# A gated-attention and feed-forward kernel on one core: its written-out order of work replaced by another, with four filler products fewer at the start

## The chip, the cores and the metric

The kernel runs on one core of a Trainium2 chip. The core has a matrix engine (PE; its weight loads are shown apart as PEld), a vector engine (DVE), an activation engine (ACT), a general engine (POOL), a queue that issues the transfers (SP), and 16 DMA engines that carry them out. The metric is the time of one execution on the device, in microseconds (us).

## What is computed

The first half is a recurrent attention over 768 steps for 4 batches of 8 heads of width 48, with a decay alpha per step and channel; the second is a feed-forward layer over the 3072 tokens (width 384, hidden width 2048) with the ELU function in between. Cut to what matters:

```python
for t in range(S):
    state = alpha[:, :, t, :, None] * state + einsum('bhd,bhe->bhde', k[:, :, t], v[:, :, t])
    y[:, :, t] = einsum('bhd,bhde->bhe', q[:, :, t], state)
x = y.transpose(0, 2, 1, 3).reshape(B * S, H * D)      # 3072 x 384
h = x @ w_in                                           # 3072 x 2048
g = np.where(h > 0, h, exp(minimum(h, 0)) - 1)
out = g @ w_out                                        # 3072 x 384
```

## The kernel before

**Windows.** The 768 steps of a batch are cut into six windows of 128 steps, 24 windows in all. In each the products of the decays are made by a scan, and the recurrence becomes a few small matrix products: scores of the queries and keys within a window, masked, and the state that is carried from window to window. The results are the columns of x.

**Token blocks and hidden blocks.** The feed-forward layer runs over nine blocks b of tokens: b = 0 to 2 have 256 tokens (two windows), b = 3 to 8 have 384 (three windows). Over the hidden width it runs in pieces j (8 of 256 columns for the first three b, 16 of 128 after that). Each 32-bit operand of these products is split into a high and a low part, and a product is made of three: high with high, high with low, low with high.

**An order written out by hand.** Every step of the program is a function with a short name (a token), and the string ORDER lists some 1,640 of them; the program is emitted in that order. Each engine carries out its own steps strictly in that order, and a step waits until what it reads is there and until the buffer that it writes is free. Two more strings say which buffers: BANKS gives, token by token, which of the eight PSUM banks a product writes, SLOTS which of eleven slots of a ring (128x512 each) holds a tile of the feed-forward layer or an output tile. A slot that held an output tile is free when the DMA that writes the output has landed. Four sets (WLV, KAV, KBV, SQV) name the windows or weights whose step runs on DVE and not on POOL, and GQ the blocks whose GL step runs on POOL and not on DVE.

The tokens that the change and the prediction's steps touch, with lines of the kernel before:

| token | engine, line | what it does |
|---|---|---|
| X.n.k, and the call X(WARM) | PE, L209 | n products of a constant tile, read by nobody (fillers); WARM of them run ahead of everything |
| L.i, LA.i, LB.i, LV.i | SP, L260 to L288 | load keys, queries and decays of window i (L whole, LA the decays, LB the rest), LV its values; the tiles for L are three, taken in turn |
| SC.i, LN.i, EX.i | DVE L300, ACT L312, L318 | scan of the decays, its logarithm, the exponential of its negative |
| KA.i, KB.i, KC.i | DVE or POOL L326, L331, DVE L336 | keys divided by the decay product, with one correction step |
| PC.i | ACT, L341 | a sum for the final check |
| TP.i (T.i later), KN.i | PE L379, ACT L409 (T: DVE L389) | transpose the keys; KN copies the result out of PSUM |
| SQ.i, S.i, MK.i | DVE or POOL L354, L357; PE L444, L428; DVE L461, L456 | queries times decays, scores, mask |
| U.i, UA.i, UB.i, UC.i | PE L491, L473; ACT L508 or DVE L510; DVE L510; DVE L539, L541 | the window's addition to the state, and the state for its second half and the next window |
| YL.i, Y3.i, Y.i, XH.i, XP.i, XL.i | PE L552, L606, L557; ACT L594, L621; PE L625; ACT or DVE | the window's results and their split into high and low |
| F.f, KW, DA, DB, WH.f, WL.f | SP L676; ACT L687; DVE L703, L708; ACT L735; DVE or POOL L755 | load weight tile f as 64-bit words, make 32-bit values of them, split these (KW, DA and DB by a pair of tiles) |
| A.b.j | PE, L787 | h for token block b and hidden piece j |
| RA, RB, RC, GH, GL (b.j) | ACT L796, L801; DVE L807; ACT L813; POOL or DVE L820 | ELU of h, its high part gh and its low part gl |
| O.b.j | PE, L836 | adds the piece's share to the output products o |
| Z.b.m | ACT L846, SP L849 | copies o out of PSUM into a ring slot, and issues the output's DMA |

The last step compares a few sums and leads to a slow general version if the inputs are out of the range for which the fast one holds; that is the same in both.

Of the kernel before, what the change touches and what calls it, by code (L numbers as in the profile page):

```python
# [61 lines left out]
YL.1 Y3.1 XP.0 Y.1 WH.2 XL.0 WH.0 F.6 MK.2 YL.2 KA.3 KB.3 KC.3 TP.3 WL.0 XH.1 KN.3 XP.1 XL.1 S.3 WL.2 F.4 KW.2 F.3
DA.2 Y3.2 LV.3 A.0.0 KW.1.1 RA.0.0 DA.1.1 F.7 F.1 DB.2 WH.6 WL.6 UB.2 DB.1.1 Y.2 XH.2 U.3 L.5 MK.3 F.5 UC.2 UA.3 PC.3
A.0.1 YL.3 WH.4 WL.4 KW.1.0 DA.1.0 RB.0.0 RC.0.0 DB.1.0 SC.5 RA.0.1 GH.0.0 UB.3 GL.0.0 L.4 RB.0.1 Y3.3 F.8 WH.1 A.0.3
RA.0.3 WL.1 WH.3 WL.3 XP.2 XL.2 F.10 RB.0.3 RC.0.1 Y.3 XH.3 LV.7 RC.0.3 UC.3 XL.3 KW.3 A.0.2 DA.3 SC.4 LN.5 A.1.1 DB.3
RA.0.2 RB.0.2 RA.1.1 EX.5 KA.5 O.0.0 RB.1.1 A.1.0 KW.4 RC.0.2 RC.1.1 RA.1.0 RB.1.0 GH.0.1 GL.0.1 GH.0.2 LN.4 F.12 DA.4
DB.4 WH.10 RC.1.0 GH.1.0 LC.1 A.1.3 KB.5 GL.1.0 WH.7 WH.8 WL.7 GH.1.1 F.9 GL.0.2 GL.1.1 A.1.2 O.0.1 RA.1.2 RB.1.2
WL.10 EX.4 O.1.0 CA.1 RC.1.2 KA.4 WH.5 WL.8 O.1.1 GH.1.2 WL.5 RA.1.3 RB.1.3 GL.1.2 A.1.5 RC.1.3 GH.0.3 F.14 ZV.6 KW.6
DA.6 CB.1 F.11 A.0.4 O.1.2 RA.0.4 RB.0.4 A.0.5 RA.1.5 O.0.2 KB.4 DB.6 WH.14 GL.0.3 SQ.4 KC.4 S.4 WH.12 RB.1.5 RA.0.5
RC.0.4 L.6 KC.5 RC.1.5 DA.5 GH.0.4 KW.5 LV.6 MK.4 TP.4 RB.0.5 GH.1.5 RC.0.5 KN.4 TP.5 KN.5 LC.3 DB.5 GH.1.3 O.0.3 PC.4  # L70
SQ.5 CA.3 LV.5 U.5 WH.9 WL.12 S.5 MK.5.1 MK.5.0 A.0.6 WH.11 WL.11 CB.3 RA.0.6 GL.1.3 O.1.3 LV.4 U.4 RB.0.6 RC.0.6 PC.5
SC.6 WL.9 LN.6 EX.6 GL.0.4 A.1.4 RA.1.4 RB.1.4 UA.4 UB.4 UC.4 L.7 SC.7 LN.7 KA.6 LC.2 RC.1.4 WL.14 A.1.6 KB.6 A.1.7
UA.5 GH.0.5 O.0.4 EX.7 KA.7 KB.7 RA.1.7 KC.6 RA.1.6 RB.1.7 RC.1.7 F.13 GH.1.4 GH.0.6 Y.5 RB.1.6 KC.7 T.7.2 GL.1.5 XH.5
Y.4 PC.7 RC.1.6 XH.4 XL.4 TP.6 GL.1.4 O.1.4 KN.6 F.15 DA.7 KW.7 O.1.5 U.6 UA.6 XL.5 DB.7 PC.6 SQ.6 S.6 MK.6.1 CA.2
GH.1.6 WH.13 GL.0.5 O.0.5 GH.1.7 L.8 UB.6 UC.6 XD.5 WL.13 GL.0.6 XD.4 LV.9 SC.8 WH.15 WL.15 MK.6.0 A.0.7 RA.0.7 GL.1.6
CB.2 RB.0.7 LN.8 EX.8 KA.8 A.2.1 T.7.3 RC.0.7 KB.8 T.7.0 KC.8 T.8.3 T.8.0 O.0.6 T.8.2 L.9 GH.0.7 A.2.0 RA.2.0 RB.2.0
LC.0 GL.1.7 O.1.6 O.1.7 Z.1.0 Z.1.1 GL.0.7 O.0.7 Z.0.0 LV.8 A.2.2 RC.2.0 RA.2.1 RB.2.1 T.7.1 GH.2.0 Z.0.1 SQ.7 U.7
RC.2.1 RA.2.2 GH.2.1 PC.8 S.7 UA.7 SQ.8 UB.7 MK.7.0 UC.7 RB.2.2 RC.2.2 GL.2.1 CA.0 S.8 SC.9 LN.9 T.8.1 EX.9 L.11 Y.6
MK.8.1 XH.6 MK.7.1 A.2.5 RA.2.5 XL.6 XD.6 GL.2.0 A.2.6 A.2.4 RA.2.4 MK.8.0 A.2.3 RB.2.5 RC.2.5 KA.9 KB.9 U.8 UA.8 Y.7
LV.11 RA.2.6 Y.8 RB.2.6 SQ.9 CB.0 GH.2.2 GL.2.2 RB.2.4 KC.9 UB.8 UC.8 GH.2.5 TP.9 KN.9 RC.2.6 XH.8 XL.8 XH.7 O.2.0  # L80
XL.7 GL.2.5 A.2.7 RC.2.4 RA.2.7 SC.11 SQ.11 U.9 LN.11 EX.11 S.9 MK.9.1 MK.9.0 RB.2.7 RC.2.7 UA.9 UB.9 UC.9 LV.10 XD.8
# [1016 lines left out]
```

## Time and profile before

| | us |
|---|---|
| median of 3 runs (464.18 to 464.94) | 464.34 |
| the profiled execution | 465.35 |
| its span, from the first to the last instruction | 463.5 |

| engine | busy us | share of the span | instructions |
|---|---|---|---|
| PE | 456.1 | 98% | 4948 |
| PEld | 440.3 | 95% | 4948 |
| DVE | 349.7 | 75% | 756 |
| ACT | 327.6 | 71% | 741 |
| POOL | 214.2 | 46% | 185 |

The span and the time of the execution differ by what lies ahead of the first and behind the last instruction. Busy time says how long an engine had an instruction in it; products on PE overlap, so the pitch from one to the next tells more than their length. In rows of the trace "out<-in" names the tile that is written and those that are read, "xN" says how many equal instructions were merged, and "[0.60 <-DVE ...]" that the engine was idle for 0.60 us just before and what ended that.

### The profile page before, as it was taken

What the parts mean: (1) busy time and instruction counts of PE and PEld (TensorE: products, weight loads), DVE (VectorE), ACT (ScalarE), POOL (GpSimd) and SP (SyncE); (2) the same over time, 40 slices, a digit from 0 to 9 for tenths busy, and PEclk for the clock granted to TensorE, in tenths of its full rate; (3) what the DMA queues carried; (4) which work ended last, traced back from release to release, by engine and by line L of the source; (5) the groups of instructions that cost most, each with busy time, mean ns of one, the idle gap of its engine ahead of it and who ended that gap; (6) DMA issues with size and microseconds to landing.
All of it is one profiled execution on the core that took longest, in us unless ns stands there. A gap on an engine that the chain in (4) does not pass through costs nothing.

```text
span 463.5 us, 12462 instructions
## 1 busy us (share of the span) xinstructions
PE 456.1 (98%) x4948; PEld 440.3 (95%) x4948; DVE 349.7 (75%) x756; ACT 327.6 (71%) x741; POOL 214.2 (46%) x185
## 2 busy tenths in 40 slices
...
GB/s 256 415 411 286 306 103 159 150 157 104 90 236 10 172 116 178 123 49 138 47 176 139 126 66 179 155 70 154 78 120 35 121 45 52 34 35 85 35 4 57
DMA packets 23715, 61.10 MB, mean 132 GB/s; under 512 B 3040, under 2 KB 10720, under 8 KB 23648
## 3 DMA queue, kind: packets, MB, share of 16 engines
...
q10 hardware_dynamic: 432, 0.59, 0.3%
...
## 4 chain that ended last, share of the span: by engine, by line
PE 88%; ACT 5%; DVE 4%; issue 1%; DMA 1%; POOL 0%; DVEq 0%; ACTq 0%; POOLq 0%
PE h L787 38%; PE o L836 38%; PE y L557 4%; PE q L428 2%; PE q L473 2%; PE wp L209 1%; PE y L552 1%; ACT w L735 1%; DVE raw L703 1%; DMA out_dram<-ot 1%; DVE wm L708 1%; ACT gh L813 1%; ACT r L801 1%; ACT r L796 1%; PE y L606 1%
## 5 line engine op out<-in xcount | busy, mean ns | idle before, releaser
L787 PE MATMUL h<-xt,w 128*128 128x384 f32 (+1 forms) x1296 | 200.1, 310 | 0.3 <-DVE r L807 0.3
L787 PEld LDWEIGHTS h<-xt,w 128*128 128x128 f32 x1296 | 190.8, 190 | 1.5 <-DVE r L807 0.4
L836 PE MATMUL o<-w,gh 128*128 128x384 f32 x768 | 188.4, 327 | 0.0
L820 POOL TENSOR_TENSOR gl<-r,gh 128x384 fp32r<-128x384 f32 (+1 forms) x90 | 106.4, 1189 | 158.7 <-ACT gh L813 104.9
L836 PEld LDWEIGHTS o<-w,gh 128*128 128x128 f32 x768 | 134.0, 189 | 0.5
L836 PE MATMUL o<-w,gl 128*128 128x384 f32 x384 | 125.3, 326 | 0.2 <-POOL gl L820 0.2
L796 ACT ACTIVATE r<-h 128x384 f32<-128x384 f32 (+1 forms) x120 | 60.5, 510 | 55.8 <-PE h L787 49.3
L389 DVE STREAM_TRANSPOSE kn<-qka 32x128 f32<-32x128 f32 x256 | 77.5, 303 | 4.2
L807 DVE SCALAR_TENSOR_TENSOR r<-r,h 128x384 f32<-128x384 f32 (+1 forms) x90 | 51.0, 577 | 38.0 <-ACT r L801 31.4
L836 PEld LDWEIGHTS o<-w,gl 128*128 128x128 f32 x384 | 72.6, 189 | 0.6 <-POOL gl L820 0.5
L801 ACT ACTIVATE r<-r 128x384 f32<-128x384 f32 (+1 forms) x120 | 64.1, 543 | 2.0
L813 ACT CAST gh<-r 128x384 fp32r<-128x384 f32 (+1 forms) x90 | 46.4, 528 | 18.6 <-DVE r L807 16.1
L357 POOL TENSOR_TENSOR st<-qka,P 64x512 f32<-64x512 f32 x34 | 43.0, 1265 | 17.4 <-DVE P L300 16.1
L456 DVE TENSOR_TENSOR st<-q,mask 64x256 f32<-64x256 f32 x76 | 32.1, 422 | 9.2 <-PE q L428 6.0
L326 POOL TENSOR_TENSOR qka<-qka,R 128x512 f32<-128x512 f32 x16 | 21.1, 1316 | 29.9 <-ACT R L318 27.8
L807 DVE SCALAR_TENSOR_TENSOR h<-r,h 128x384 f32<-128x384 f32 (+1 forms) x30 | 17.5, 589 | 21.0 <-ACT r L801 20.5
L300 DVE TENSOR_TENSOR_SCAN P<-qka,first 128x516 f32<-128x516 f32 (+1 forms) x25 | 31.0, 1244 | 0.5 <-DMA qka<-in_qka_dram 0.2
L820 DVE TENSOR_TENSOR gl<-h,gh 128x384 fp32r<-128x384 f32 (+1 forms) x30 | 17.3, 582 | 18.2 <-ACT gh L813 7.7
L726 ACT ACTIVATE ck<-ck,lim 128x384 f32<-128x384 int32 x32 | 25.5, 795 | 0.6
L721 ACT ACTIVATE ck<-ck,lim 128x384 int32<-128x384 int8 x32 | 25.3, 792 | 0.0
L312 ACT ACTIVATE R<-P 128x512 f32<-128x512 f32 (+1 forms) x25 | 15.4, 615 | 11.4 <-DVE P L300 11.3
L813 ACT CAST gh<-h 128x384 fp32r<-128x384 f32 (+1 forms) x30 | 14.8, 497 | 8.8 <-DVE h L807 7.2
...
## 6 DMA issues: line engine op xcount, KB each, us to landing
qka<-in_qka_dram SPq DMA_DIRECT2D x18, 770.0 KB, 5.5
...
```

The source lines that it names most:

```text
L300: nc.vector.tensor_tensor_scan(out=P[:, n].rearrange("p n w -> p (n w)"), data0=t[:, 2 * NP * W + n.start * AW:2 * NP * W + n.stop * AW], ...
L357: eng(SQV, i).tensor_tensor(out=st[r, a], in0=d["q"][r], in1=pw(i)[r], op=ALU.mult)
L389: nc.vector.transpose(out=kn[32 * t:32 * t + 32, :, 32 * g:32 * g + 32], in_=d["kt"][32 * g:32 * g + 32, :, 32 * t:32 * t + 32])
L456: nc.vector.tensor_tensor(out=d["st"][r, a, :, c * C:(c + 1) * C], in0=d["s4"][a][o], in1=mask[o].unsqueeze(1).broadcast_to([64, NP, C]), ...
L726: nc.scalar.activation(out=t[:, :, 1].bitcast(F32), in_=t[:, :, 0], func=AF.Square, bias=lim[:, 1:2], accum_out=chk_w[:, f:f + 1])
L787: nc.tensor.matmul(h[:, y, :], lhsT=t[:, wi, ws], rhs=x[:, c, xi].rearrange("p (a x) -> p x a", a=2), start=(y == 0 and k == 0), stop=(k = ...
L796: nc.scalar.activation(out=r, in_=d["h"], func=AF.Relu, scale=-1.0)
L801: nc.scalar.activation(out=d["r"], in_=d["r"], func=AF.Exp, scale=-1.0)
L807: nc.vector.scalar_tensor_tensor(out=d["g"], in0=d["r"], scalar=-1.0, in1=d["h"], op0=ALU.add, op1=ALU.max)
L813: nc.scalar.copy(out=gh, in_=d["g"])
L820: q.tensor_tensor(out=gl, in0=d["g"], in1=d["gh"].bitcast(F32), op=ALU.subtract)
L836: nc.tensor.matmul(o[:, 0:DM], lhsT=gt[:, y, ms], rhs=t[:, wi, f * DM:f * DM + DM].rearrange("p (a x) -> p x a", a=2), start=(u == 0 and y ...
```

## The change

WARM goes from 17 to 13. ORDER, BANKS and SLOTS are replaced as a whole, and the sets that divide work between DVE and POOL are replaced with them. The functions are the same. The new ORDER is one line longer, which shifts the code below it by one: L326 before is L327 after. Of the tables a line or two:

```diff
-WARM = 17
+WARM = 13
...
-WLV, KAV, KBV, SQV = (0, 2, 7, 8, 10, 11, 13, 15),  \
-    (0, 1, 2, 3, 6, 7, 14, 22),  \
-    (0, 1, 2, 3, 4, 7, 11, 22, 23),  \
-    (0, 1, 18, 19)
+WLV, KAV, KBV, SQV = (0, 7, 8, 10, 11, 13, 15),  \
+    (0, 1, 2, 3, 7, 14, 18, 19, 22, 23),  \
+    (0, 1, 2, 3, 4, 6, 7, 22, 23),  \
+    (0, 1, 18, 21, 23)
...
 ORDER = """
-LA.0.0 SC.0.0 LN.0.0 EX.0.0 LA.0.1 SC.0.1 LB.0.0 LN.0.1 KA.0.0 LV.0.0 KB.0.0 EX.0.1 KC.0.0 TP.0.0 KA.0.1 KB.0.1 KC.0.1
-PC.0 X.4.1 TP.0.1 KN.0 LA.1 SC.1 LB.1.1 LB.0.1 LN.1 X.4.2 U.0 SQ.1 SQ.0 EX.1 S.0 LB.1.0 KA.1 KB.1 KC.1 X.2.0 UC.0 L.2
+LA.0.0 SC.0.0 LN.0.0 EX.0.0 LA.0.1 SC.0.1 LB.0.0 LA.1 KA.0.0 KB.0.0 LN.0.1 KC.0.0 EX.0.1 KA.0.1 KB.0.1 TP.0.0 LV.0.0
+X.4.1 KC.0.1 PC.0 LB.1.1 LB.0.1 TP.0.1 KN.0 X.3.2 U.0 SC.1 SQ.1 LN.1 LB.1.0 SQ.0 S.0 EX.1 KA.1 KB.1 X.2.0 KC.1 PC.1
...
 BANKS = """
-7012345671205364721567305216401732542014564164514514516545614561420763542107563475423616142302147350
+7012345671205364721563407521632475603247517417547574517457415757415326041726053760475317542312476302
...
 SLOTS = """
-0123456789a042356718904625783a6918a0564904672013a56829734a065872130694a27565704981324756243185706967
+0123456789a135607241a5690738146a928a17595a16039247a815629738a15420683249a754a12349608297824076934671
```

What this moves, at three places. The names are those of the program; a number behind a tile's name only tells tiles apart.

SP, the queue of transfers, from the first weight tiles on. qka is the input of a window (L), vs the values (LV; 128x384 is a half), raw a weight tile (F). Before:

```order
L676 DMA raw_278<-in_wgt_dram 128x6141 x2
L260 DMA qka_128<-in_qka_dram 128x1540
L285 DMA vs_114<-in_vv_dram 128x768
L285 DMA vs_113<-in_vv_dram 128x384
L676 DMA raw_432<-in_wgt_dram 128x6141 x2
L676 DMA raw_478<-in_wgt_dram 128x6141
L285 DMA vs_115<-in_vv_dram 128x768
```

After:

```order
L677 DMA raw_282<-in_wgt_dram 128x6141 x2
L261 DMA qka_124<-in_qka_dram 128x1540
L286 DMA vs_109<-in_vv_dram 128x384
L286 DMA vs_110<-in_vv_dram 128x768
L677 DMA raw_437<-in_wgt_dram 128x6141
L286 DMA vs_111<-in_vv_dram 128x768
L677 DMA raw_437<-in_wgt_dram 128x6141
L677 DMA raw_454<-in_wgt_dram 128x6141
```

L.3 (the second row) keeps its place; the half LV.1.1 and LV.2 behind it change places, and LV.3 moves up between the weight tiles F.4 and F.6.

DVE, from the state of window 2 to the keys of window 3. P is the scan of window 3, wm the weights of pair 0, st the masked scores and vs the state of window 2. Before:

```order
L541 SCALAR_TENSOR_TENSOR vs_114<-u,P 128x192
L703 TENSOR_SCALAR raw_278<-raw_278 128x768
L708 SCALAR_TENSOR_TENSOR wm<-raw_278 128x768
L300 SCALAR_TENSOR_TENSOR P<-qka_128,first 128x516
L708 SCALAR_TENSOR_TENSOR wm<-raw_278 128x768
L510 TENSOR_TENSOR vs_114<-vs_114,q 128x192
L461 TENSOR_TENSOR st<-sc,mask 128x2x4x64
L326 TENSOR_TENSOR qka_128<-qka_128,R 128x512
```

After:

```order
L542 SCALAR_TENSOR_TENSOR vs_110<-u,P 128x192
L709 SCALAR_TENSOR_TENSOR wm<-raw_282 128x768
L704 TENSOR_SCALAR raw_282<-raw_282 128x768
L301 SCALAR_TENSOR_TENSOR P<-qka_124,first 128x516
L462 TENSOR_TENSOR st<-sc,mask 128x2x4x64
L511 TENSOR_TENSOR vs_110<-vs_110,q 128x192
L709 SCALAR_TENSOR_TENSOR wm<-raw_282 128x768
L327 TENSOR_TENSOR qka_124<-qka_124,R 128x512
```

The number of steps ahead of the scan (SC.3) and of the keys (KA.3) is the same; the state step (UA.2) now stands ahead of the second weight step, and the mask (MK.2) ahead of both.

ACT, from the results of windows 4 and 5 (y, xt) to the state of window 6 (vs). kn is the copy of window 6's transposed keys, raw with 128x1536 the cast of weight pair 7. Before:

```order
L620 ACTIVATE y_1367,chk_y<-y 128x128
L621 ACTIVATE xt,chk_y<-y 128x3x128
L409 COPY kn<-tp 128x512
L687 ACTIVATE raw_1296<-raw_1296 128x1536
L508 ACTIVATE vs_114<-q 48x192 x2
```

After:

```order
L621 ACTIVATE y_1360,chk_y<-y 128x128
L622 ACTIVATE xt,chk_y<-y 128x3x128
L814 CAST gh<-r 128x512
L688 ACTIVATE raw_1325<-raw_1325 128x1536
L410 COPY kn<-tp 128x512
L509 ACTIVATE vs_110<-q 48x192 x2
```

A gh and the cast of the weight pair now stand ahead of the copy of the keys.

## Rows read from the trace of the kernel before

**Rows 1.** Stages: us; busy us (instructions) by engine; granted clock; DMA share; GB/s.
```profile
15.00:20.00 5.00, 5.00 (x106) 4.41 (x106) 4.83 (x9) 4.46 (x12) 1.05 (x1) 1.00 1.02 407
...
60.00:70.00 10.00, 10.00 (x102) 9.71 (x102) 9.98 (x9) 9.09 (x14) 9.34 (x6) 1.00 0.45 120
```

**Rows 2.** The chain that ended last: start us, us, what.
```profile
1.07 6.78 PE wp L209 x17
...
451.57 7.33 PE o L836 x45
```

**Rows 3.** PE's waits: us in total, times, longest us.
```profile
PE tp L379 <- DVE qka L336: 0.6, 1, 0.6
PE y L606 <- ACT y L594: 0.3, 1, 0.3
PE h L787 <- DVE r L807: 0.3, 1, 0.3
PE q L473 <- DMA vs<-in_vv_dram: 0.3, 1, 0.3
PE o L836 <- POOL gl L820: 0.2, 1, 0.2
```

**Rows 4.** PE's weight loads in order of time: start us, us.
```profile
7.02 0.34 PEld L209 LDWEIGHTS <-wz 128*128 128x128 bf16 x2 [0.28 <-issue]
7.48 0.36 PEld L379 LDWEIGHTS tp<-ident,qka 128*128 128x128 f32 x2
```

**Rows 5.** DVE in order of time: KC.0.0, KC.0.1, SC.3, DB.0.0, KA.3, KC.3.
```profile
6.01 0.42 DVE L336 SCALAR_TENSOR_TENSOR qka<-R,qka 128x256 f32<-128x256 f32 x1
...
7.27 0.42 DVE L336 SCALAR_TENSOR_TENSOR qka<-R,qka 128x256 f32<-128x256 f32 x1
...
20.23 1.23 DVE L300 TENSOR_TENSOR_SCAN P<-qka,first 128x516 f32<-128x516 f32 x1
21.38 0.93 DVE L708 SCALAR_TENSOR_TENSOR wm<-raw 128x768 int32<-128x768 int32 x1
...
23.09 0.81 DVE L326 TENSOR_TENSOR qka<-qka,R 128x512 f32<-128x512 f32 x1
...
24.66 0.69 DVE L336 SCALAR_TENSOR_TENSOR qka<-R,qka 128x512 f32<-128x512 f32 x1
```

**Rows 6.** PE in order of time: TP.1, U.2, TP.3, the first h behind S.3.
```profile
13.30 0.66 PE L379 MATMUL tp<-ident,qka 128*128 128x128 f32 x4 [0.60 <-DVE qka L336]
...
21.27 0.68 PE L473 MATMUL q<-vs,kn 64*64 64x48 f32 x32 [0.27 <-DMA vs<-in_vv_dram]
...
25.83 0.66 PE L379 MATMUL tp<-ident,qka 128*128 128x128 f32 x4
...
27.66 2.27 PE L787 MATMUL h<-xt,w 128*128 128x256 f32 x18
```

**Rows 7.** SP in order of time: the issue of L.3.
```profile
12.21 0.33 SPq L260 DMA_DIRECT2D qka<-in_qka_dram  x1
```

**Rows 8.** Transfers issued from 12.2 to 12.4 us: count, KB each, us to landing.
```profile
qka<-in_qka_dram SPq DMA_DIRECT2D x1, 770.0 KB, 8.0
```

**Rows 9.** Line L849, the output's transfers from 313 to 325 us.
```profile
DMA to landing us min/median/max: 1.9/4.1/4.3
```

**Rows 10.** ACT and PE in order of time: two gh, kn.6, KW.7; U.6.
```profile
85.93 1.14 ACT L813 CAST gh<-r 128x512 fp32r<-128x512 f32 x2
...
90.26 0.58 ACT L409 COPY kn<-tp 128x512 f32<-128x512 f32 x1
90.73 2.45 ACT L687 ACTIVATE raw<-raw 128x1536 int32<-128x1536 uint8 x1
...
93.91 0.57 PE L473 MATMUL q<-vs,kn 64*48 64x48 f32 x32
```

**Rows 11.** PE in order of time: the last o ahead of an island of small products.
```profile
334.35 0.33 PE L836 MATMUL o<-w,gl 128*128 128x384 f32 x1
334.61 0.57 PE L473 MATMUL q<-vs,kn 64*48 64x48 f32 x32
```

More of the change, by code (lines that the diff above doesn't have):

```diff
@@ L62 @@
[L62 to L81, printed above, removed]
@@ new lines @@
+A.1.3 RC.1.0 KA.5 KB.5 RB.1.1 RC.1.1 GL.0.2 WH.8 GH.1.0 LN.4 GL.1.0 O.0.0 O.0.1 WH.10 WL.10 O.1.0 GH.1.1 GL.1.1 O.1.1
+EX.4 KA.4 RB.1.2 RC.1.2 RA.1.3 RB.1.3 WH.7 GH.1.2 WL.8 WH.5 WL.7 LV.7 GL.1.2 RC.1.3 LC.1 CA.1 WL.5 KB.4 ZV.6 LV.4 CB.1
+F.14 KW.6 LV.6 SQ.4 GH.0.3 L.6 DA.6 DB.6 A.1.5 RA.1.5 GL.0.3 RB.1.5 A.0.4 RA.0.4 RB.0.4 A.0.5 KC.4 F.9 KW.5 SQ.5
+RC.0.4 O.0.2 WH.12 WL.12 PC.4 RA.0.5 RB.0.5 KC.5 O.1.2 RC.1.5 LC.3 S.4 PC.5 TP.4 KN.4 DA.5 TP.5 MK.4 KN.5 RC.0.5
+GH.0.4 CA.3 GH.0.5 GH.1.3 DB.5 O.0.3 WH.11 CB.3 LV.5 U.5 S.5 MK.5.1 MK.5.0 WH.9 GL.0.4 WL.11 A.0.6 U.4 UA.4 UB.4
@@ new lines @@
+RB.2.7 RC.2.7 S.9 MK.9.0 GL.2.6 KA.11 KB.11 KC.11 T.11.2 PC.11 O.2.1 GH.2.4 GL.2.4 O.2.2 LV.11 A.3.0 A.3.3 RC.2.3
+A.3.2 LC.4 SC.10 MK.9.1 GH.2.3 LV.10 T.11.3 T.11.0 GH.2.5 GL.2.3 LN.10 EX.10 A.3.1 KA.10 KB.10 RA.3.1 A.3.6 RA.3.6
+KC.10 T.10.3 T.10.1 RB.3.6 CA.4 CB.4 PC.10 O.2.3 A.3.4 GL.2.5 SQ.11 RA.3.4 L.12 RA.3.3 RB.3.4 O.2.4 O.2.5 RB.3.3
+GH.2.7 T.10.0 SC.12 RA.3.2 RB.3.1 RA.3.0 RC.3.1 GL.2.7 T.10.2 O.2.6 O.2.7 RB.3.2 RC.3.2 RB.3.0 RC.3.0 LN.12 GH.3.1
+GH.3.0 SQ.10 T.11.1 Z.2.0 RC.3.6 EX.12 Z.2.1 U.10 LC.5 S.10 GL.3.1 MK.10.1 MK.10.0 UA.10 RC.3.4 S.11 RC.3.3 U.11 KA.12
@@ new lines @@
+GL.3.0 MK.11.0 A.3.7 MK.11.1 RA.3.7 RB.3.7 GH.3.3 A.3.5 RA.3.5 RB.3.5 KB.12 KC.12 O.3.0 L.14 GH.3.4 O.3.1 RC.3.5 LV.12
+GH.3.2 GL.3.2 A.3.8 CA.5 L.13 GH.3.5 GL.3.5 UB.10 T.12.3 UC.10 A.3.14 O.3.2 PC.12 RA.3.8 SQ.12 RB.3.8 UA.11 RC.3.7
+GH.3.7 RC.3.8 GL.3.3 T.12.2 T.12.1 GL.3.7 T.12.0 Y.10 XH.10 XL.10 CB.5 Y.11 XH.11 Y.9 LV.13 XL.11 GL.3.4 RA.3.14
+RB.3.14 XD.11 O.3.3 O.3.4 A.3.10 SC.13 SQ.13 U.12 LN.13 EX.13 GH.3.8 RC.3.14 GL.3.8 S.12 KA.13 MK.12.1 GH.3.6 UA.12
+A.3.11 MK.12.0 UB.12 O.3.5 UC.12 LC.7 XH.9 XL.9 A.3.9 KB.13 RA.3.11 RB.3.11 RA.3.10 RB.3.10 RA.3.9 RB.3.9 A.3.12
@@ new lines @@
+A.3.15 RC.3.10 RC.3.11 GL.3.6 O.3.6 CA.7 O.3.7 RA.3.12 RC.3.9 RB.3.12 SC.14 LN.14 EX.14 SQ.14 KC.13 XD.9 ZV.12 T.13.0
+GH.3.9 GL.3.9 KA.14 T.13.2 KB.14 O.3.8 GH.3.11 RC.3.12 XD.10 O.3.9 RA.3.15 A.4.3 A.4.1 RB.3.15 RC.3.15 GH.3.10 KC.14
+L.15 GL.3.10 O.3.10 GL.3.11 T.13.3 CB.7 O.3.11 T.14.2 RA.4.3 RB.4.3 T.13.1 GH.3.12 U.13 GH.3.14 RC.4.3 GH.4.3 S.13
+GL.3.14 GL.3.12 UA.13 MK.13.0 LC.6 CA.6 MK.13.1 T.14.3 CB.6 A.3.13 GH.3.15 GL.3.15 RA.3.13 RB.3.13 RC.3.13 A.4.0
+RA.4.0 RB.4.0 T.14.0 LV.15 RC.4.0 T.14.1 O.3.12 UB.13 UC.13 GH.3.13 A.4.4 GL.3.13 GH.4.0 O.3.13 LC.9 PC.13 GL.4.3
@@ new lines @@
+MK.15.1 UA.15 LN.16 UB.15 GH.4.8 EX.16 KA.16 UC.15 GH.4.7 Y.14 XH.14 LV.18 GH.4.5 O.4.4 GL.4.5 CB.10 XD.12 SC.17
+GL.4.8 LV.17 A.4.9 RA.4.9 XL.14 GL.4.7 MK.15.0 KB.16 KC.16 T.16.1 T.16.3 O.4.5 GH.4.6 T.16.2 GL.4.6 A.4.10 SQ.17
+T.16.0 RA.4.10 RB.4.9 RB.4.10 LN.17 RC.4.9 EX.17 KA.17 A.4.11 KB.17 RC.4.10 O.4.6 LC.11 CA.11 A.4.15 RA.4.11 A.4.14
+RA.4.14 CB.11 RB.4.11 XD.14 KC.17 GH.4.12 T.17.1 O.4.7 O.4.8 GH.4.9 GL.4.9 GH.4.10 GL.4.10 PC.16 PC.17 A.5.1 O.4.9
+RC.4.11 GH.4.13 LV.16 L.18 SC.18 LN.18 GH.4.11 LC.12 GL.4.11 T.17.0 U.16 RA.5.1 S.16 MK.16.1 O.4.10 EX.18 KA.18
@@ new lines @@
+O.5.1 KC.19 LC.14 T.19.2 T.19.1 CA.14 A.5.6 XD.15 LV.19 T.19.3 CB.14 RA.5.6 A.5.5 RA.5.5 RB.5.5 A.5.11 T.19.0 A.5.9
+RA.5.9 O.5.2 RC.5.5 GH.5.4 RB.5.9 RC.5.9 GL.5.3 O.5.3 RA.5.8 RB.5.8 GL.5.4 RC.5.8 GH.5.5 GL.5.5 O.5.4 LC.15 GH.5.7
+GL.5.7 RB.5.6 T.18.1 CA.15 L.20 S.18 U.18 CB.15 UA.18 LC.16 MK.18.1 Y.17 XH.17 LV.21 UB.18 O.5.5 RC.5.6 MK.18.0
+RA.5.11 RB.5.11 RC.5.11 GH.5.6 GH.5.8 A.5.10 GL.5.8 GL.5.6 U.19 XL.17 S.19 PC.19 GH.5.9 GL.5.9 UC.18 MK.19.1 UA.19
+UB.19 A.5.15 RA.5.15 O.5.6 RA.5.10 O.5.7 GH.5.11 MK.19.0 A.5.14 SC.20 A.5.13 LN.20 GL.5.11 RB.5.15 EX.20 RC.5.15
@@ new lines @@
+GH.5.15 RA.5.13 KA.20 RA.5.14 KB.20 UC.19 O.5.8 O.5.9 L.22 KC.20 T.20.3 A.5.12 CA.16 XD.17 CB.16 RB.5.13 XD.16 A.6.0
+RB.5.10 PC.20 RC.5.10 RB.5.14 RC.5.14 RA.5.12 GH.5.10 GL.5.10 A.6.3 RC.5.13 RB.5.12 L.21 T.20.0 RC.5.12 LC.17 GH.5.12
+T.20.1 O.5.10 GL.5.15 RA.6.0 O.5.11 GL.5.12 A.6.1 RB.6.0 SQ.20 SC.21 CA.17 SQ.21 O.5.12 GH.5.14 GH.5.13 GL.5.13
+GL.5.14 O.5.13 O.5.14 O.5.15 RC.6.0 CB.17 LN.21 EX.21 KA.21 KB.21 RA.6.3 T.20.2 RA.6.1 RB.6.3 RC.6.3 KC.21 RB.6.1
+T.21.2 LC.18 T.21.0 U.20 CA.18 CB.18 S.20 UA.20 UB.20 LC.19 UC.20 Y.19 GH.6.0 GL.6.0 Z.5.0 A.6.9 T.21.1 Z.5.1 A.6.5
```

132 lines of the change are left out of this document (59 added, 73 removed), and 6 rows, old and new, of the table GQ.

## The prediction

> **What bounds the kernel now.** I read the stages first, then PE's waits, the chain that ended last, and last the instructions in order of time at the few places that those point to. In the stages PE is busy all the time, and in the first 80 us so is nearly everything else: at 15 to 20 us the DMA engines are at a share of 1.02 with 407 GB/s, at 60 to 70 us DVE works 9.98 of 10 us and ACT 9.09 [rows 1]. A busy PE is not yet a PE at its peak, so I looked at the pitch: 45 products of o take 7.33 us on the chain, 0.163 us each, which is 384 columns at 2.4 GHz (0.160) and a little [rows 2]. So where PE runs the products of h and o it has nothing to give. What a new order can change is (a) the filler products ahead of the first transposes, (b) the waits, of which PE shows only 1.7 us behind the fillers, and 1.2 us of it before 23.2 us [rows 3], and (c) how often PE goes from wide products to the small ones and back. All terms below are therefore small, and the reader should expect a result within 1 or 2 us; a measurement of this kernel can tell about 0.2% (0.93 us) from no change.
>
> The profiled execution took 465.35 us: 463.5 of span and 1.85 around it. That is 1.0 us above the median of 464.34. I take every term as a difference against that execution and put the sum on the median.
>
> **Fillers and the way to 27.7 us.** Seventeen fillers start at 1.07 [rows 2]. The sixteenth and seventeenth loads stand at 7.02, the first transposes' load at 7.48 [rows 4]; as the first two loads stand together at 1.07, the pitch until then is (7.02 - 1.07)/14 = 0.425 us, 512 columns at 1.2 GHz. Thirteen end at 1.07 + 13 x 0.425 = 6.60. The first transposes need KC.0.0, which ends at 6.01 + 0.42 = 6.43, so they can start at 6.60 and the four removed fillers are worth 7.48 - 6.60 = 0.88 us there. The second pair of transposes needs KC.0.1, which begins at 7.27 [rows 5] and cannot end before 7.69. From there the order is as before (kn copy, LN.1, EX.1, KA.1, KB.1, KC.1), so I take 0.6 us of the 0.88 to arrive at KC.1, and TP.1 starts at 12.7 and not at 13.30 [rows 6]. PE still waits for it, as it did.
>
> Now the point on which this prediction stands: what is late next. Window 3's input (L.3) is issued at 12.21 [rows 7] and lands 8.0 us later [rows 8], at 20.2; SC.3 on DVE starts at 20.23 [rows 5]. Its issue waits for S.0, and that comes earlier, but the queue in front of it is full, 407 GB/s at a share of 1.02 [rows 1], and the same 12 transfers stand ahead of it. So I keep 20.2. DVE has the same steps to do between KC.1 and SC.3 as before, comes there 0.6 us early and waits. From SC.3 on I follow the new order: the copy of yl.1 now stands ahead of LN.3 on ACT, and on DVE UA.2 stands ahead of the second weight step (DB.0.1), which stands ahead of KA.3. UA.2 needs U.2, U.2 needs LV.2; before, U.2 started at 21.27 when LV.2 had landed [rows 6]; LV.1.1 (192 KB, 0.47 us at 407 GB/s) now stands ahead of LV.2, so U.2 starts at some 21.7, takes 0.7, UA.2 is done at 22.75. Its twin DB.0.0 took 0.93 [rows 5], so KA.3 starts at 23.7; KA.3 to KC.3 took from 23.09 to 24.66 + 0.69 = 25.35 before [rows 5], 2.26 us, so KC.3 ends at 25.9. Before, PE came to TP.3 at 25.83 without waiting [rows 6]; now it comes some 0.8 us early and waits until 25.9. TP.3, the correction and S.3 then end at 27.75 against 27.66 [rows 6]. So the 0.88 us are 0.6 at 12.7 us and nothing at 27.7: **+0.1**. Ends of the range: -0.6 (all that arrives at TP.1 stays) and +0.5 (U.2 or DB.0.1 slips as far as LV.1.1's 0.47).
>
> **PE's other waits.** Two lie behind 27.7 us. At 78 us an h waits for its PSUM bank (0.3 shown, DVE's r [rows 3]): in the new order the bank of that block (A.1.4) was last read by UA.4, one DVE step some 2 us earlier in the order than RC.0.6 was. I take it as gone. At 321 us an o waits for gl (0.2 [rows 3]); its gh stood in a ring slot that an output tile had held, and ACT waited for the output DMA, which lands up to 4.3 us after its issue [rows 9]. In the new order I counted the products that PE has between an output's last o and the first o that uses a block in one of its slots, at 0.163 us each: 10 us at the least, where the stretch at 321 us had 6.5. The DMA takes 4.3 of that. Gone as well. Rows give -0.5 for both; the modelled ends hide some of each wait, so -0.9 is the far end. I take **-0.6**.
>
> **A new wait.** On ACT the two casts that prepare weight pair 7 (KW.7) and a gh now stand ahead of kn.6. Before, kn.6 began at 90.26 and ended at 90.84, KW.7 (2.45) followed, and U.6, the first to need kn.6, began at 93.91 [rows 10]. With a gh (0.57, half of the pair at 85.93 [rows 10]) and KW.7 ahead, kn.6 ends at 90.26 + 0.57 + 2.45 + 0.58 = 93.9. That is the moment PE wants it: **+0.1**, from 0 to +0.7 by what ACT has queued ahead.
>
> **Islands of small products.** Going from o to a small product costs 334.61 - 334.35 = 0.26 instead of 0.163 [rows 11], going back about as much again. Counted over PE's order there are 26 such islands and no longer 27, the rest is the same products: **-0.2**.
>
> **Work moved between engines.** KA, KB, SQ, WL and GL change between DVE and POOL for a score of tiles, ACT has the same steps as before. PE is the cover of all of it: outside of the waits above it did not wait for DVE even where DVE worked 9.98 of 10 us [rows 1]. I set this at nothing; where the cover goes, PE waits for one of those engines, and that is the third rival.
>
> Sum: +0.1 - 0.6 + 0.1 - 0.2 = -0.6: 464.75 beside the profiled execution, **463.7** at the median.
>
> **The clock.** [...] The fillers' pitch is that of 1.2 GHz until 7.02, and the next two take half of it [rows 4]; PE had been busy without a gap for 5.95 us when that changed. With 13 fillers the transposes and four more fillers follow at once, so I leave the change at 7.0 and add nothing. [...] No run here shows yet what fewer fillers do to it; rival 4 is that case.
>
> **Rivals.**
> 1. The front keeps its gain. L.3 is issued up to 0.7 us earlier; if its slowest engine takes it up as much earlier, SC.3, KC.3 and TP.3 move with it and the front is -0.6. Then 463.7 - 0.7 = 463.0. For it: SC.3 starts at the landing and nothing else. Against it: the share of 1.02. Chance 0.27.
> 2. The change does not do what it says: the waits at 78 and 321 us are replaced by others of their size (+0.6) and the front stays at +0.1: 463.7 + 0.6 = 464.3. This is the upper half of the forecast's own range.
> 3. Slower: kn.6 behind KW.7. The gh ahead of KW.7 waits for its RC on DVE, and DVE is full there. If a DVE step of 2 us stands in between, or the pair's second half lands late (its issue waits until the spare tile is free), KW.7 starts 2 us late and all of it is exposed: PE waits for kn.6. It decides at 91.0 us: each us that KW.7 begins later than that is a us of PE. Price 1.9, so 463.7 + 1.9 = 465.6. For it: KW.7 and the gh are 3.0 us of work that ACT did not have ahead of kn.6 before. Against it: PE's slack there was 93.91 - 90.84 = 3.1 us [rows 10]. Chance 0.16.
> 4. The clock rises some us later. The four fillers behind the first transposes then take 0.425 and not 0.216, 0.84 us in all, which puts TP.1 back to 13.5, and the first small products run at half speed too: +0.5 at 27.7 instead of +0.1, 464.1. Chance 0.05.
>
> **Numbers.** The forecast (rival 2 within it) has 0.52 and its own range 463.1 to 464.5; about 0.12 of that lies below 463.4, the border of "faster by over 0.2%". Rival 1 lies below it in nine cases of ten. So faster 0.12 + 0.24 = 0.36, slower (over 465.27) 0.14 from rival 3 and 0.03 from waits that I did not see, 0.17, the rest 0.47 within 0.2%. The range takes rival 1's lower half with the far end of the waits (463.0 - 0.4) and rival 3 down to its likelier half: 462.6 to 465.4.
>
> **What would show it.** In the timeline of the changed kernel: first transposes at 6.6; TP.1 near 12.7; SC.3 again at 20.2 and a wait of PE of 0.5 to 1 us ahead of TP.3 at 25 to 26 us; no wait for an output DMA on ACT; the first small products after the kn.6 copy at 93 to 95 us, with a wait of at most 0.7. If SC.3 starts at 19.6, rival 1 is right. If PE waits more than 1 us for ACT's kn at about 93 us, rival 3 is. The prediction is wrong in its kind if PE shows waits of over 1 us behind 100 us, where I read none out of the order, or if the pitch of the wide products is not 0.163.

## The result, and the profile after

| | before | after |
|---|---|---|
| median of 5 runs, us | 464.86 (464.18 to 464.94) | 466.82 (466.80 to 467.33) |
| profiled execution, us | 465.35 | 466.82 |
| its span; end of PE's last product | 463.5; 458.88 | 465.1; 460.61 |

The change makes the kernel slower: ratio 1.0056, interval 1.0046 to 1.0067 (the ratios here and below are those on record, each with its 95% interval; they are not the quotients of the two medians, here 1.0042). The forecast was 463.7 (462.6 to 465.4), with 0.17 on slower.

PE's waits in the changed kernel, against [rows 3] (us in total, times, longest; the wait ahead of the fillers, 1.1 us in both, is left out in both):

```profile
PE yl L553 <- DVE vs L511: 0.9, 1, 0.9
PE q L474 <- PE h L788: 0.8, 1, 0.8
PE y L553 <- issue: 0.7, 1, 0.7
PE tp L380 <- DVE qka L337: 0.6, 1, 0.6
PE h L788 <- DVE r L808: 0.3, 1, 0.3
PE q L474 <- DVE st L457: 0.2, 1, 0.2
```

The waits for values (q for vs), for Y3.1's copy, for the bank at 78 us and for gl at 321 us are gone. In their place stand three that are longer. PE in order of time shows where (start us, us, what):

```profile
22.28 1.07 PE L553 MATMUL y<-st,vs 48*48 48x64 f32 x29
24.08 0.71 PE L553 MATMUL y<-st,vs 48*48 48x64 f32 x17 [0.74 <-issue]
...
25.30 0.66 PE L380 MATMUL tp<-ident,qka 128*128 128x128 f32 x4
...
35.36 0.73 PE L553 MATMUL yl<-st,vs 48*64 48x64 f32 x16 [0.95 <-DVE vs L511]
36.02 2.27 PE L788 MATMUL h<-xt,w 128*128 128x256 f32 x18
...
76.65 0.28 PE L474 MATMUL q<-vs,kn 64*64 64x48 f32 x2 [0.77 <-PE h L788]
77.15 0.67 PE L474 MATMUL q<-vs,kn 64*64 64x48 f32 x30 [0.22 <-DVE st L457]
...
285.80 1.41 PE L788 MATMUL h<-xt,w 128*128 128x384 f32 x7 [0.31 <-DVE r L808]
```

In order: a stop in the middle of Y.1 (at 23.1; the expectations below call the step Y.2), then TP.3 (25.30); YL.3 waits for UA.3 (35.36); U.4 waits for the banks of S.5 (76.65 and 77.15); A.5.10 waits for its bank (285.80).

To see what each costs in the end, I counted the products of h and o in the order of the program and compared the start of the same step in both traces:

| PE's start of | before | after | difference |
|---|---|---|---|
| A.0.3 | 35.38 | 36.02 | +0.63 |
| A.0.6 | 72.97 | 73.60 | +0.63 |
| A.1.6 | 80.22 | 81.81 | +1.60 |
| A.2.7 | 128.77 | 130.37 | +1.60 |
| end of the last product | 458.88 | 460.61 | +1.73 |

These differences are 0.82 us too small. The profiled execution of the kernel before is 1.0 us above the 464.34 of the earlier runs, and in it KC.1 began at 12.55, in that of the changed kernel at 11.73. This start differs from execution to execution: in the three other traces of the old order (experiments 10 to 12 below, which change nothing ahead of it but the fillers) it stands at 11.84 with 17 fillers, and at 11.55 and 12.47 with 13. What makes it differ was not found. Counted from KC.1, A.0.3 starts after 22.83 to 22.84 us in all four traces of the old order, and after 24.29 in the changed kernel. So the change is 1.46 us late at A.0.3, another microsecond goes at 76 us, and behind 100 us a wait gone (321) and a new one (285) nearly balance. That makes 2.55 us at the end, which fits the ratio (0.56% of 464.3 us are 2.6); the medians give 1.96 with the 464.86 of the table and 2.48 with the 464.34 of the earlier runs. The lead that the changed kernel seems to have ahead of 35 us is the late start of the other execution.

Who is late is DVE. Up to MK.5.0 it has the same steps in both orders, but for WL.2, which the change gives to POOL. Yet it is 0.8 us early at KC.1 and 1.7 late at MK.5.0, so it loses 2.5 us in between. DVE in the changed kernel (SC.3, DA.2, DB.2, DB.1.1, MK.3, UA.3; then DB.5 and MK.5):

```profile
19.67 1.22 DVE L301 TENSOR_TENSOR_SCAN P<-qka,first 128x516 f32<-128x516 f32 x1
...
25.72 1.99 DVE L704 TENSOR_SCALAR raw<-raw 128x1536 int32<-128x1536 int32 x1
...
28.80 2.07 DVE L709 SCALAR_TENSOR_TENSOR spare<-raw 128x1536 int32<-128x1536 int32 x1 [0.22 <-ACT raw L688]
...
32.01 2.43 DVE L709 SCALAR_TENSOR_TENSOR spare<-raw 128x768 int32<-128x768 int32 x1 [0.54 <-ACT w L736]
34.37 0.68 DVE L462 TENSOR_TENSOR st<-sc,mask 128x512 f32<-128x512 f32 x1
34.97 0.34 DVE L511 TENSOR_TENSOR vs<-vs,q 128x192 f32<-128x192 f32 x1
...
72.56 2.67 DVE L709 SCALAR_TENSOR_TENSOR spare<-raw 128x1536 int32<-128x1536 int32 x1
75.26 1.75 DVE L457 TENSOR_TENSOR st<-q,mask 64x256 f32<-64x256 f32 x4
```

POOL beside it (WL.2, WL.6, two GL):

```profile
25.07 1.82 POOL L756 TENSOR_TENSOR w<-wm,w 128x768 fp32r<-128x768 f32 x1 [2.87 <-DVE qka L337]
31.81 1.82 POOL L756 TENSOR_TENSOR w<-spare,w 128x768 fp32r<-128x768 f32 x1 [4.92 <-ACT w L736]
...
72.18 1.29 POOL L821 TENSOR_TENSOR gl<-r,gh 128x512 fp32r<-128x512 f32 x1 [1.78 <-ACT gh L814]
73.90 2.47 POOL L821 TENSOR_TENSOR gl<-r,gh 128x512 fp32r<-128x512 f32 x1 [0.42 <-ACT gh L814]
```

The same steps of DVE before (DB.1.1; DB.5, MK.5):

```profile
31.50 0.95 DVE L708 SCALAR_TENSOR_TENSOR spare<-raw 128x768 int32<-128x768 int32 x1
...
71.75 1.81 DVE L708 SCALAR_TENSOR_TENSOR spare<-raw 128x1536 int32<-128x1536 int32 x1
73.59 1.75 DVE L456 TENSOR_TENSOR st<-q,mask 64x256 f32<-64x256 f32 x4
```

and of POOL:

```profile
32.27 4.12 POOL L755 TENSOR_TENSOR w<-spare,w 128x768 fp32r<-128x768 f32 x2 [8.92 <-ACT w L735]
...
72.00 2.73 POOL L820 TENSOR_TENSOR gl<-r,gh 128x512 fp32r<-128x512 f32 x1 [2.37 <-ACT gh L813]
```

Read the two pairs side by side. DB.1.1 takes 0.95 where it begins 0.77 us ahead of POOL's WL; after, WL.6 begins 0.2 ahead of it and it takes 2.43, ending 0.81 behind WL.6's end (34.44 and 33.63). DB.5 takes 1.81 where it begins 0.25 ahead of a GL, which then takes 2.73; after, the GL begins first and takes 1.29, and DB.5 takes 2.67, ending 1.76 behind it. It reads as if the two could not run at once. That was the theory for the runs, with two rivals: the missing fillers cost (A), and a wait that is taken away comes back at the next one (B).

### The profile page after: what moved, and what is told of

The parts are those of the page before. It is cut to its first block, busy times and chain, and to the rows that moved or that the text cites. A ratio compares the mean times of both kernels' runs of the same rounds, so it can differ in the third digit from the quotient of the medians.

```text
span 465.1 us, 12452 instructions
## 1 busy us (share of the span) xinstructions
PE 455.8 (98%) x4943; PEld 440.3 (95%) x4943; DVE 355.5 (76%) x760; ACT 329.1 (71%) x741; POOL 205.5 (44%) x181
## 5 line engine op out<-in xcount | busy, mean ns | idle before, releaser
L821 POOL TENSOR_TENSOR gl<-r,gh 128x384 fp32r<-128x384 f32 (+1 forms) x89 | 101.2, 1144 | 186.5 <-ACT gh L814 112.5
L390 DVE STREAM_TRANSPOSE kn<-qka 32x128 f32<-32x128 f32 x256 | 77.5, 303 | 4.2
L358 POOL TENSOR_TENSOR st<-qka,P 64x512 f32<-64x512 f32 x32 | 41.9, 1309 | 13.9 <-DVE P L301 9.7
L327 POOL TENSOR_TENSOR qka<-qka,R 128x512 f32<-128x512 f32 x14 | 19.2, 1371 | 13.1 <-ACT R L319 9.3
L337 DVE SCALAR_TENSOR_TENSOR qka<-R,qka 128x512 f32<-128x512 f32 (+1 forms) x25 | 18.7, 749 | 3.4 <-POOL R L332 3.1
```

The source lines that it names most:

```text
L358: eng(SQV, i).tensor_tensor(out=st[r, a], in0=d["q"][r], in1=pw(i)[r], op=ALU.mult)
L390: nc.vector.transpose(out=kn[32 * t:32 * t + 32, :, 32 * g:32 * g + 32], in_=d["kt"][32 * g:32 * g + 32, :, 32 * t:32 * t + 32])
L821: q.tensor_tensor(out=gl, in0=d["g"], in1=d["gh"].bitcast(F32), op=ALU.subtract)
```

## The experiments

Edits are to the changed kernel unless it says otherwise; each was measured beside the kernel before on the same chip. The intervals are 95%.

**1. Seventeen fillers again.**

```diff
-WARM = 13
+WARM = 17
```

> The changed kernel with 17 fillers again. Theory (the new waits at 34, 76 and 285 us cost the time, the front does not): the first transposes and TP.1 go back by 0.9 us, the first h by 0.5 to 0.9, so 467.2 to 467.7, slower than the change by 0.1 to 0.2%; the stop in the middle of Y.2 at 23.1 us (0.95 us), if PE is there ahead of its code, shrinks to 0.3 us or less, because PE comes 0.9 us later to a block of instructions that arrives when it did. Rival A (the four missing fillers are what costs, by the clock or otherwise): at most 465.9. Rival (the stop at 23.1 us is a wait for data in the order): it stays 0.9 us long and moves to 24.0.

466.83, ratio 1.0050 (1.0036 to 1.0063): the time of the change. PE in order of time:

```profile
22.37 1.75 PE L553 MATMUL y<-st,vs 48*48 48x64 f32 x47
...
25.29 0.63 PE L380 MATMUL tp<-ident,qka 128*128 128x128 f32 x4 [0.64 <-issue]
...
35.36 0.73 PE L553 MATMUL yl<-st,vs 48*64 48x64 f32 x16 [1.32 <-DVE vs L511]
```

Four fillers more, and KC.1 (11.82, in the change 11.73), TP.3 (25.30 in the change) and YL.3 (35.36) start at nearly the same moments; PE only waits elsewhere. Rival A falls. My figure for the front missed (nothing instead of 0.4 to 0.9). The stop in Y.1 has shrunk to 0.24 us, as expected if PE is there ahead of its code; the section on the hardware comes back to it.

**2. The state of window 3 first.** MK.3 and UA.3 move up on DVE.

```diff
-U.3 DA.1.1 KW.1.1 DB.1.1 WL.2 A.0.1 RA.0.1 L.5 Y3.2 MK.3 WH.6
+U.3 MK.3 UA.3 DA.1.1 KW.1.1 DB.1.1 WL.2 A.0.1 RA.0.1 L.5 Y3.2 WH.6
...
-F.1 UA.3 DA.1.0
+F.1 DA.1.0
```

> The changed kernel with MK.3 and UA.3 moved ahead of DA.1.1 and DB.1.1 on DVE. Theory (YL.3 waits at 35.4 us because UA.3 stands behind DB.1.1, which took 2.43 us beside a WL on POOL): the wait of 0.95 us ahead of YL.3 is gone, and if nothing takes its place 465.7 to 466.0. Rival B (a wait taken away comes back at the next one down, DB.1.1 and the weights behind it being late instead): 466.6 to 467.0, with a new wait of about 1 us between 36 and 60 us.

466.33, 1.0045 (1.0031 to 1.0059). The wait ahead of YL.3 is gone and A.0.3 starts 1.51 us earlier than in the change, but 0.5 of it is gone by A.1.1 (a wait of 0.28 shows at 41.8 us) and 0.6 more by A.0.6 at 73; 0.57 is left at the end of the trace, and 0.49 by the medians, which is less than their intervals. Rival B is two thirds right: DVE behind is nearly as late as it was (DB.5 begins at 72.33 and not at 72.56).

**3 and 4. Two ways to free U.4.** First U.4 behind O.1.3 again (with banks 4 and 7 exchanged from A.1.4 on), then DB.5 behind MK.5.

```diff
-A.0.6 U.4 UA.4 UB.4 RA.0.6
+A.0.6 RA.0.6
...
-GL.1.3 O.1.3 L.7
+GL.1.3 O.1.3 U.4 UA.4 UB.4 L.7
```

> The changed kernel with U.4, UA.4 and UB.4 behind O.1.3 as before, and banks 4 and 7 exchanged from A.1.4 on, so that A.1.4 takes the bank of A.0.6. Theory (U.4 needs the banks of S.5, which MK.5 reads late because DB.5 took 2.67 us beside a GL on POOL; two us of o between S.5 and U.4 covered that): the waits of 0.77 and 0.22 us at 76.7 and 77.2 are gone, A.1.4 waits 0.3 to 0.5 for RC.0.6 as it did before: 465.8 to 466.3. Rival B: 466.6 to 467.0.

467.59, 1.0068 (1.0055 to 1.0082).

```diff
-GH.1.3 DB.5 O.0.3 WH.11 CB.3 LV.5 U.5 S.5 MK.5.1 MK.5.0 WH.9
+GH.1.3 O.0.3 CB.3 LV.5 U.5 S.5 MK.5.1 MK.5.0 DB.5 WH.11 WH.9
```

> The changed kernel with DB.5 and WH.11 moved behind MK.5.0, U.4 left where the change put it. Theory: MK.5 then starts when S.5 ends (73.7 us) and is done at 75.5, so U.4 starts at 75.6 to 75.8 without its waits of 1.0 us: 465.6 to 466.0, if the weights of pair 5 are not needed within 2 us. Rival B: O of piece 5 or A.1.6 waits for those weights instead, 466.6 to 467.2.

467.20, 1.0054 (1.0040 to 1.0067). Neither is faster than the change (1.0056), and both forecasts of the theory missed. PE waits elsewhere: in the first A.1.4 waits 0.45 for RC.0.6 and S.6 at 96 us 0.7 for XL on DVE; in the second A.1.4 waits 1.19 for UA.4. Rival B is right for these: where DVE is late, moving what waits for it only moves the wait.

**5. WH.6 behind PC.3 on ACT.** Two neighbours change places; POOL's WL.6 starts later.

```diff
-Y3.2 MK.3 WH.6 PC.3 WL.6
+Y3.2 MK.3 PC.3 WH.6 WL.6
```

> The changed kernel with WH.6 behind PC.3 on ACT, two neighbours exchanged, so that WL.6 on POOL can start at 32.4 us and not at 31.8. Theory (from 28 to 97 us DVE sets the pace, and a step of DVE between two SBUF tiles stands still while a step of POOL that began first runs): DB.1.1 then starts at 31.6, before WL.6, and takes 0.95 to 1.05 us and not 2.43; MK.3 and UA.3 end 1.4 to 1.9 earlier, the wait ahead of YL.3 is gone or below 0.2, and 0.5 to 1.0 us are left of it at the end: 465.8 to 466.3. Rival (DB.1.1 is slow for its own sake, or waits for something on ACT): DB.1.1 stays over 2 us and the time at 466.8. Rival B (all comes back at the next wait): DB.1.1 is short, the time 466.6 or more.

465.79, 1.0030 (1.0020 to 1.0040). DVE and POOL:

```profile
31.82 0.97 DVE L709 SCALAR_TENSOR_TENSOR spare<-raw 128x768 int32<-128x768 int32 x1 [0.54 <-DVE raw L704]
32.70 0.69 DVE L462 TENSOR_TENSOR st<-sc,mask 128x512 f32<-128x512 f32 x1
33.30 0.35 DVE L511 TENSOR_TENSOR vs<-vs,q 128x192 f32<-128x192 f32 x1
```

```profile
31.98 4.69 POOL L756 TENSOR_TENSOR w<-spare,w 128x768 fp32r<-128x768 f32 x2 [5.03 <-ACT w L736]
```

DB.1.1 now begins 0.16 us ahead of WL.6 and takes 0.97; the two WL, 1.82 each when alone, take 4.69. MK.3 and UA.3, which read PSUM, run at their usual length beside them (0.69 and 0.35). PE no longer waits for YL.3, A.0.3 comes 1.62 earlier, and 1.49 of it is kept to the end of the trace (1.0 by the medians). The theory holds, and rival B does not here: DVE itself is earlier.

**6. GH.0.4 behind CA.3 on ACT.**

```diff
-GH.0.4 CA.3 GH.0.5
+CA.3 GH.0.4 GH.0.5
```

> The changed kernel with GH.0.4 behind CA.3 on ACT, two neighbours exchanged, so that GL.0.4 on POOL starts at 72.9 and not at 72.18. Theory: DB.5 on DVE (72.56) then comes first, takes 1.8 us and not 2.67, MK.5 ends at 76.1 and not at 77.0, and the waits of PE at 75.6 to 77.2 fall from 1.2 us in all to 0.4: 466.0 to 466.4. In return that GL on POOL takes 2.5 us and not 1.29. Rival (the length of DB.5 does not come from POOL): 2.6 us and 466.8.

466.36, 1.0037 (1.0024 to 1.0051). DVE's DB.5 begins first and takes 1.81; the two GL take 3.94:

```profile
73.45 1.81 DVE L709 SCALAR_TENSOR_TENSOR spare<-raw 128x1536 int32<-128x1536 int32 x1
```

```profile
73.71 3.94 POOL L821 TENSOR_TENSOR gl<-r,gh 128x512 fp32r<-128x512 f32 x2 [2.43 <-ACT gh L814]
```

U.4's first wait is gone, its second (0.2) stays; from A.0.6 to A.1.6 PE needs 0.78 us less than in the change. By the medians 0.46 is left; the interval touches that of the change, so the size rests on the trace.

**7. Both exchanges.**

> The changed kernel with both exchanges. Theory: the two gains follow one another on the same engine and mostly add up: 465.0 to 465.8, with PE not waiting for YL.3 and less than 0.5 us at 75 us. Rival B: no better than the better of the two alone.

464.93, 1.0012 (1.0003 to 1.0021): they add up (1.0 and 0.5 alone, 1.9 together, the surplus within the intervals). The profiled execution is the slowest of this run, 468.26 where the others took 464.37 to 465.52, and shows why so little decides: there WL.6 began 0.04 us ahead of DB.1.1 (32.37 and 32.41), which took 2.60.

```profile
32.41 2.60 DVE L709 SCALAR_TENSOR_TENSOR spare<-raw 128x768 int32<-128x768 int32 x1 [0.54 <-ACT w L736]
```

```profile
32.37 4.32 POOL L756 TENSOR_TENSOR w<-spare,w 128x768 fp32r<-128x768 f32 x2 [5.17 <-ACT w L736]
```

By experiment 5 that is worth some 1.5 us, half of what this execution is above the median (3.3). The other half is the clock. PE waited 1.50 us for YL.3, up to 35.92; from 37.4 to 40.7 us the granted clock reads 0.50, and the 18 products of A.0.3, 2.27 us in the change, take 3.57. A stage of this execution (us; busy us by engine; granted clock; DMA share; GB/s) and A.0.3 in it:

```profile
37.40:40.70 3.30, 3.30 (x20) 3.08 (x20) 3.27 (x6) 1.14 (x4) 0.00 (x0) 0.50 1.02 419
```

```profile
36.58 3.57 PE L788 MATMUL h<-xt,w 128*128 128x256 f32 x18
```

In experiment 1 PE waited 1.32 us at the same place, and the granted clock stayed at 1.00. That the wait brought the clock down is not tested.

**8. RC.5.6 ahead of MK.18.1 on DVE.**

```diff
-LC.16 MK.18.1 Y.17 XH.17 LV.21 UB.18 O.5.5 RC.5.6 MK.18.0
+LC.16 RC.5.6 MK.18.1 Y.17 XH.17 LV.21 UB.18 O.5.5 MK.18.0
```

> The changed kernel with RC.5.6 ahead of MK.18.1 on DVE. Theory: A.5.10 takes the PSUM bank that RC.5.6 frees; DVE idles 1.9 us ahead of MK.18.1 at 283.5, so RC.5.6 costs nothing there and the wait of 0.5 us at 285.2 goes for good, because behind 100 us DVE is not the bound: 466.2 to 466.5. Rival B: 466.8.

466.28, 1.0035 (1.0021 to 1.0048). The wait at 285 us is gone, and the 0.48 us that PE wins there is kept (0.58 at the end of the trace, 0.54 by the medians; here too the interval touches that of the change).

**9. The three exchanges of 5, 6 and 8 together.**

> The changed kernel with the three exchanges that helped: WH.6 behind PC.3, GH.0.4 behind CA.3, RC.5.6 ahead of MK.18.1. Theory: the first two take back the 1.6 us that PE loses by 81 us, the third the 0.5 at 285: 464.2 to 464.6, the time of the kernel before within 0.2%. Rival (something else of the new order costs as well): 465.0 or more.

464.33, ratio to the kernel before 1.0001 (0.9992 to 1.0010). PE's waits:

```profile
PE y L553 <- issue: 0.7, 1, 0.7
PE tp L380 <- DVE qka L337: 0.6, 1, 0.6
PE tp L380 <- issue: 0.3, 1, 0.3
PE q L474 <- DVE st L457: 0.2, 1, 0.2
PE q L474 <- PE h L788: 0.2, 1, 0.2
```

Three exchanges of neighbouring steps, none of which changes what an engine has to do, give back all that the change had cost: 466.82 - 464.33 = 2.5 us. So its price lies in these three places. The rest of the new order (the fillers, the two waits that are gone, the new division of work between DVE and POOL, all of which this version keeps) is in sum worth nothing either way, within 0.1%. Counted from KC.1, A.0.3 starts here after 22.81 us, as in the old order.

**10. The kernel before without its two late waits.**

```diff
-A.0.6 WH.11 WL.11 CB.3 RA.0.6 GL.1.3 O.1.3 LV.4 U.4 RB.0.6 RC.0.6 PC.5
+A.0.6 WH.11 RA.0.6 GL.1.3 O.1.3 LV.4 U.4 RB.0.6 CB.3 RC.0.6 WL.11 PC.5
...
-MK.20.0 LV.21 Z.5.1 GH.6.3 Y.19 Z.5.2 XH.19
+MK.20.0 Z.5.1 GH.6.3 Y.19 Z.5.2 LV.21 XH.19
```

> The kernel before with its two late waits taken away by hand: on ACT CB.3 behind RB.0.6 and on DVE WL.11 behind RC.0.6, so that A.1.4 finds its bank free at 77.6; on SP LV.21 behind Z.5.2, so that the output tiles of block 5 land 2 us and not 4.3 us after their issue and GL.6.0 finds its slot. Theory: 0.4 to 0.5 us at 77.6 and 0.3 at 321, both kept, as nothing on DVE or ACT is late behind them: 463.5 to 463.9. Rival B: WL.11 comes late instead, 464.3 or more.

465.46, 1.0031 (1.0019 to 1.0043): slower, and the theory's own mechanism did it. The wait at 321 us is gone and 0.46 us with it, A.1.4 finds its bank; but the later WL.11 pushed SC.6 behind a WL on POOL, and UA.4 stands behind SC.6. DVE, POOL and PE:

```profile
77.61 2.85 DVE L300 TENSOR_TENSOR_SCAN P<-qka,first 128x516 f32<-128x516 f32 x1
```

```profile
76.83 2.55 POOL L755 TENSOR_TENSOR w<-wm,w 128x768 fp32r<-128x768 f32 x1
```

```profile
80.76 1.49 PE L787 MATMUL h<-xt,w 128*128 128x256 f32 x11 [1.47 <-DVE vs L510]
```

The scan, 1.23 alone [rows 5], took 2.85 and ended 1.08 behind the WL.

**11 and 12. Thirteen fillers in the order before, alone and with the edit of 10.**

> The kernel before with 13 fillers, nothing else. Theory: PE is there 0.9 us early at the first transposes; the block of instructions that it needs at 24 us and the state of window 3 on DVE (33.8 us; YL.3 came 0.9 us behind it at 34.7) are not earlier, so 0.3 to 0.6 of the 0.9 arrive at A.0.3 and less behind U.4 (MK.5 was done 1.8 us ahead of U.4): 463.7 to 464.2. Rival A (fewer fillers cost, by the clock): 464.5 or more. Rival (the front keeps everything): 463.5.

464.39, 1.0009 (1.0000 to 1.0019).

> The kernel before with the two waits taken away and with 13 fillers. Theory: the gains of the two add up, 463.0 to 463.7, faster than either kernel. Rival B: no better than the better of the two, 463.6 or more.

465.53, 1.0027 (1.0019 to 1.0036). Both forecasts missed. Four fillers fewer are worth nothing in the old order either: no gain beyond what can be told, and no cost. No version here is faster than the kernel before.

## Why the prediction was wrong

- **The step that failed** is the one on work moved between engines: "PE is the cover of all of it ... I set this at nothing". It took "PE did not wait" for a cover without measuring the cover. The trace of before had it: UA.3 ended at 33.77 and YL.3 started at 34.73, 0.96 us of cover; MK.5 ended at 75.34 (its row is shown above) and U.4 started at 77.13, 1.79. UA.3, YL.3 and U.4 before:

```profile
33.42 0.35 DVE L510 TENSOR_TENSOR vs<-vs,q 128x192 f32<-128x192 f32 x1
...
34.73 0.73 PE L552 MATMUL yl<-st,vs 48*64 48x64 f32 x16
...
77.13 0.68 PE L473 MATMUL q<-vs,kn 64*64 64x48 f32 x32
```

  Counted from KC.1, UA.3 ended 2.34 us later in the change than before, more than the 0.96 could take; with DB.1.1 short (experiment 5) it ended 0.65 later, and PE did not wait. DVE was full in [rows 1], so anything that made one of its steps longer came through. The change took WL.2 from DVE, a gain by the count of steps, and moved others so that POOL came first in two meetings: 1.48 us at DB.1.1 (2.43 against 0.95) and 0.86 at DB.5 (2.67 against 1.81), beside 1.0 at DA.2, which DB.2's wait for KW.2 hid. And it put U.4 ahead of O.1.3, which took 2 us of cover away from the second. Experiment 7 sizes the two places: 466.82 - 464.93 = 1.9 us that the term should have held. Experiments 8 and 9 say the same, 466.28 - 464.33 = 1.95, or 1.7 when each is set against the runs of the kernel before beside it (464.44 and 464.21).
- **The front** (+0.1) was reasoned wrongly, and that the first h came at 27.59 against 27.66 before, close to the forecast, is luck: that execution had begun KC.1 0.82 us earlier. The prediction took DVE to wait for L.3 and SC.3 to start at its landing. In the trace of before DVE was busy until then:

```profile
19.36 0.96 DVE L708 SCALAR_TENSOR_TENSOR wm<-raw 128x768 int32<-128x768 int32 x1
```

  L.3 landed at 20.2, this step ended at 20.32, and SC.3 followed it without idle time (the records of DVE overlap by some 0.09 us). In the changed kernel L.3 landed 7.0 us after an issue at 11.39, at 18.4, and SC.3 began only at 19.67, again straight behind a step of DVE. SC.3 starts 7.68 or 7.69 us after KC.1 in the four traces of the old order and 7.94 or more after it in the ten of the new, so the front of the new order is if anything slower. Rival 1's sign (SC.3 at 19.6) came up without its mechanism. Of the 0.6 us that the prediction let the missing fillers win at KC.1, experiment 1 shows 0.09 (11.82 with 17 fillers, 11.73 with 13), and experiments 1, 11 and 12 show that the four fillers are worth nothing in either order.
- **PE's two waits** at 78 and 321 us (-0.6) are gone as forecast. I had not looked for their successors: A.5.10's wait at 285 (0.48 us by experiment 8) costs as much as the one at 321 did (0.46 by experiment 10), which is rival 2 by half. Of the -0.6 and of the -0.2 for an island fewer nothing is left in sum: experiment 9, which keeps both, takes the time of the kernel before. The island that is gone lay between 28 and 38 us, where DVE set the pace, and no run prices it by itself.
- **kn.6 behind KW.7** (+0.1): right. The copy ended at 95.25 and U.6 started at 95.51, straight behind the last o, 1.6 us late with everything else. Rival 3 was the right kind at the wrong place: a step behind a slowed DVE or ACT step, but at MK.5 and UA.3.
- **The clock**: the mean granted clock of the run is 0.999, and in its trace it reads 1.00 from 7 to 12 us; the four fillers behind the first transposes took 1.03 us, as in the trace of before, so rival 4 did not happen. The prediction's 1.2 and 2.4 GHz stand for columns per ns: in the trace of before the fillers' 512 columns took 0.427 us ahead of 7 us (1.2) and 0.216 behind it (2.4), and the 384 of an o take 0.163 (2.36). The traces give the granted clock as a share alone; that the slower pitch was one of the clock is the prediction's reading.
